# Threshold attention and an MLP mixer on one core: identity turns that wait for a bank, and second-layer visits of 256 features

## The chip, the core and the metric

The kernel runs on one core of a Trainium2 chip. The metric is the device time of one execution in microseconds (us). The engines go by their short names: PE is TensorE (matrix products; PEld is its weight loads), DVE is VectorE, ACT is ScalarE, POOL is GpSimd, SP is the engine whose queue starts most transfers. All data are f32. A matrix product of f32 shows in the profile as two PE instructions ("passes"), each with its own weight load, so that 12 products are 24 passes.

## What is computed

Attention with a threshold (B=8 rows, H=8 heads, S=576 tokens, D=64), then a mixer on the 8 rows of 576 tokens by 512 features:

```python
scores = scale * q @ k.T                         # per row and head
scores = where(scores >= max(scores) - tau, scores, -1e9)
x = softmax(scores) @ v                          # heads side by side: (8, 576, 512)
h = relu(x.T @ w_tok1) @ w_tok2                  # token layers: 576 -> 256 -> 576
u = x + h.T
out = u + relu(u @ w_ch1) @ w_ch2                # channel layers: 512 -> 1536 -> 512
```

## The kernel before

**Stages.** The rows go through attention one after the other. While PE does the attention of row b+1, it also does the token layers and one or two channel groups of row b; that other work fills PE where attention waits for ACT, DVE or POOL. A channel group is 256 tokens of one row through both channel layers. `NOW` (L524) says how many groups of a row are done in this way: two of row 0, one of each of rows 1 to 6, none of row 7, eight in all. The rest is done at the end, from 903 us on, by `class Late` (L1250), in another scheme with 256-wide products; the diff doesn't touch it.

**A channel group** (`make_groups`, L919). First layer: 12 visits (`ch1`, L944), each 4 products of 128x128 weights by 256 tokens into one bank, then a relu on ACT (L953) or DVE (L956) into `g`. Second layer: `ch2` (L958). A visit takes 128 tokens `t` and 128 output features `c`; it is 12 products, one for each block `j` of the hidden layer: the weights are a 128x128 block of `g`, and what is streamed is 128 columns of `wc2` (L964). In row 0 a product with the identity ahead of them adds `u` (L962). A group has 2 x 4 = 8 such visits. `leave` (L973) takes the bank out: in row 0 a copy on ACT (L984), in the other rows an addition on DVE (L978) of the bank and of `ut`, which holds u turned to tokens by features; then `store` (L986) writes 128 tokens to `out`, once the four visits of a `t` have left. `ut` comes from `turn_u`, a DVE transpose (L933) into the buffer `us`, which must wait until the stores of the group before have read `us`, and from four moves in SP's queue (L940).

**Banks.** A visit to PE that leaves something in PSUM needs a bank. Until attention ends there are two, `m0` and `m1` (L707); two more come afterwards (L1216). Who needs one: the turns of attention's weights in row 0 (L300), attention's value products (L365, L370), the token layers (L435, L454, L472) and both channel layers. The scores (L825) have banks of their own.

**The order of the work** is written by a planner at build time (`class Scheduler`, L568 on). Every piece of work is an `Op` with an engine, a cost in us, a function that emits its instructions, what it depends on, and a rank (low goes first). `banked` (L591) makes two: the visit on PE, which takes a bank as it starts, and its leaving, which gives the bank back 0.15 us after its end. The planner keeps one clock for each engine and emits, over and over, the piece that can start first; among those that PE can start now, `pick` (L617) puts first those whose inputs and bank have been there for about a microsecond (`sure`, L598: a piece on the same engine counts 0.2 us after the end of what it needs), then the lowest rank. Ranks on PE: value products 0, scores 1 (-1 in row 0), token layers 1.5, or 2.5 right after another token piece, channel layers 2. A round of scores is moreover held back while the other work done so far, `self.done` (L694: the costs of banked visits that belong to a row), is below the round's due value (`planned_at`, L1165, worked out with `GROUP` = 41.8 for a group), as long as something else can start. On the chip each engine then works through its own instructions in the emitted order.

**Turns of the identity** (`keep_warm`, L647). Before a piece is put on PE that starts before 110 us of the planner's clock (`WARM_UNTIL`, L550), the gap ahead of it is filled with transposes of the identity that nobody reads. There are as many as fit in the gap less `WARM_GAP` = 0.6 us, at 0.11 us each. They need a bank, and are left out if none is free at the moment at which PE's gap begins.

Of the kernel before, what the change touches and what calls it, by code (L numbers as in the profile page):

```python
# [17 lines left out]
P = 128  # L18
# [3 lines left out]
def kernel(  # L22
# [38 lines left out]
    NCC = DM // P  # L61
    NJ = DCH // P
# [7 lines left out]
    work = ctx.enter_context(tc.tile_pool(name="work", bufs=2))  # L70
# [74 lines left out]
    wc2 = const.tile([P, NJ, DM], F32, name="wc2")  # L145
# [233 lines left out]
    class Step:  # L379


        def __init__(self, kind, cost, on, cost_out, work, leave, other=None):
            self.kind, self.cost, self.on, self.cost_out, self.work, self.leave = kind, cost, on, cost_out, work, leave
            self.other = other
# [167 lines left out]
    class Op:  # L552

        def __init__(self, eng, cost, fn, deps, after, rank, lag, row, index):
            self.eng, self.cost, self.fn, self.rank, self.lag, self.row, self.index = eng, cost, fn, rank, lag, row, index
            self.end, self.bank, self.frees, self.later, self.open, self.other = None, None, None, [], 0, None
            self.dmas, self.landed, self.shared = None, None, False
            self.deps = [d for d in deps if d is not None]
            for d in self.deps + [d for d in after if d is not None]:
                if d.end is None:  # L560
                    d.later.append(self)
                    self.open += 1
# [5 lines left out]
    class Scheduler:  # L568
# [22 lines left out]
        def banked(self, cost, work, on, cost_out, leave, deps=(), rank=5, row=None, rank_out=0, other=None):  # L591
            x = self.op("pe", cost, work, deps, rank, row=row)
            y = self.op(on, cost_out, leave, (x,), rank_out, row=row, other=other)
            x.bank = True
            y.frees = x
            return x, y

        def sure(self, x):  # L598
            t = max([d.landed + SPARE if d.landed else d.end + d.lag + SLACK * (d.eng != x.eng) for d in x.deps] + [0.0])
            if x.bank:  # L600
                t = max(t, min(b.free for b in self.banks if b.free is not None) + SLACK)
            return t
# [44 lines left out]
        def keep_warm(self, t):  # L647

            now = self.clock["pe"]
            banks = [b for b in self.banks if b.free is not None and b.free <= now]  # L650
            n = int((t - now - WARM_GAP) / WARM_TURN)
            if not banks or n < 1 or not now:
                return
            b = banks[0]
            to = b.pool.tile([P, MAIN], F32, tag=b.tag, name=f"warm_{len(self.warmed)}")
            for _ in range(n):
                nc.tensor.transpose(out=to[:, 0:P], in_=ident, identity=ident)
            self.clock["pe"] = now + n * WARM_TURN
            b.free = self.clock["pe"] + 0.15
            self.warmed.append((now, n))  # L660

        def run(self, until):
            while not until():
                best = None
                for e in self.clock:
                    c = self.pick(e)
                    if c and (best is None or c[0][0] < best[0][0]):
                        best = c + (e,)
                if best is None:
                    assert all(x.end is not None for x in self.ops), [(x.eng, x.rank, x.index, x.open) for x in self.ops if x.end is None][:20]  # L670
                    return
                _, t, x, eng = best
                if eng == "pe" and t < WARM_UNTIL:
                    self.keep_warm(t)
                self.ready[x.eng].remove(x)
                if x.other:
                    self.ready[x.other[0]].remove(x)
                    if eng != x.eng:
                        x.eng, x.cost, x.fn = x.other
                if x.dmas:  # L680
                    x.end = self.transfer(t, *x.dmas)
                    x.landed = self.in_flight[-1]
                else:
                    x.end = t + x.cost
                self.clock[x.eng] = x.end
                if x.eng == "pe":
                    self.last_rank = x.rank
                if x.bank:
                    b = min((b for b in self.banks if b.free is not None), key=lambda b: b.free)
                    b.free = None  # L690
                    x.bank = b, b.pool.tile([P, MAIN], F32, tag=b.tag, name=f"bank_{x.index}")
                    x.fn(x.bank[1])
                    if x.row is not None:
                        self.done += x.cost  # L694
                elif x.frees:
                    b, tile_ = x.frees.bank
                    x.fn(tile_)
                    b.free = x.end + 0.15
                else:
                    x.fn()  # L700
                for y in x.later:
                    y.open -= 1
                    if not y.open:
                        self.enter(y)

    sched = Scheduler()
# [3 lines left out]
    def key_op(*key):  # L710
        return keyed.get(key)
# [165 lines left out]
    fills = {}  # L877
# [41 lines left out]
    def make_groups(b, halves):  # L919
        uT = xTs[b]  # L920
        reads = []
        for i in range(NOW[b]):
            s = {}
            n, nt = GR, GR // P

            def new_us(s=s, i=i):
                s["us"] = work.tile([P, nt, 4, NCC * 32], F32, tag="us", bufs=1, name=f"us_{b}_{i}")
# [27 lines left out]
            def relu_v(bank, j, s=s):  # L955
                nc.vector.tensor_scalar(out=s["g"][:, j, 0:n], in0=bank[:, 0:n], scalar1=0.0, scalar2=None, op0=ALU.max)  # L956

            def ch2(bank, t, c, s=s, i=i):  # L958
                to = bank[:, 0:P]
                t0 = GR * i + P * t  # L960
                if not b:
                    nc.tensor.matmul(to, lhsT=uT[:, c, t0 : t0 + P], rhs=ident, is_transpose=True, start=True, stop=False, skip_group_check=True)  # L962
                for j in range(NJ):
                    nc.tensor.matmul(  # L964
                        to,
                        lhsT=s["g"][:, j, P * t : P * t + P],
                        rhs=wc2[:, j, P * c : P * c + P],
                        start=(j == 0 and b > 0),
                        stop=(j == NJ - 1),
                        skip_group_check=True,  # L970
                    )

            def leave(bank, t, c, s=s):  # L973
                if not b and "us" not in s:
                    new_us(s)
                o = s["us"][:, t].rearrange("q a x -> q (a x)")[:, P * c : P * c + P]
                if b:
                    nc.vector.tensor_add(  # L978
                        out=o.rearrange("q (k d) -> q k d", k=4),
                        in0=bank[:, 0:P].rearrange("q (k d) -> q k d", k=4),  # L980
                        in1=s["ut"][:, t][:, :, 32 * c : 32 * c + 32],
                    )
                else:
                    nc.scalar.copy(out=o, in_=bank[:, 0:P])  # L984
# [12 lines left out]
            for j in range(NJ):  # L997
                x, y = sched.banked(
                    1.79,
                    lambda bank, j=j, f=ch1: f(bank, j),  # L1000
                    "act",
                    0.29,
                    lambda bank, j=j, f=relu: f(bank, j),
                    have + state["ch2"] + [key_op("pool", 7 + j)],
                    2,
                    b,
# [5 lines left out]
            seconds, stores, adds = [], [], []  # L1012
            for t in range(nt):
                outs = []
                for c in range(NCC):
                    x, y = sched.banked(
                        2.7 if b else 2.8,
                        lambda bank, t=t, c=c, f=ch2: f(bank, t, c),
                        "dve" if b else "act",
                        0.21,  # L1020
                        lambda bank, t=t, c=c, f=leave: f(bank, t, c),
                        relus + moved + (converted if not b else []) + (state["stores"] if not b else []),
                        2,
                        b,
                        1 if b else 0,
                    )
                    outs.append(y)
                    seconds.append(x)
                    if not b:
                        reads.append(x)  # L1030
                    fills[b] = fills.get(b, 0.0) + x.cost
                adds += outs
                stores.append(sched.op("sp", 0.35, lambda t=t, f=store: f(t), outs, 2, dmas=(1, 150, 0.35)))
            state["ch2"], state["stores"], state["adds"] = seconds, stores, adds
# [453 lines left out]
```

## Time and profile before

| | us |
|---|---|
| three runs: median (lowest to highest) | 1270.09 (1269.9 to 1276.9) |
| the profiled execution: its own time | 1273.39 |
| its span, from the first to the last instruction | 1271.4 |
| PE busy in the span | 1237.8 |
| DVE, ACT, POOL busy | 755.0, 564.0, 315.4 |
| mean granted clock of PE | 0.991 of full |
| end of the last second-layer visit | 903.3 |

Lines of the profile name the engine, the source line (L964 is the product of `ch2`), the tile written and the tiles read. A timeline line is: start, length, engine, line, operation, what is written and read, how many, and in brackets the idle time ahead of it with what ended it. The table of windows gives, for each stretch of time, its length, then the busy time and number of instructions of PE, PEld, DVE, ACT and POOL, then PEclk, the share of the full clock that PE was granted, then DMA's share and GB/s. The chain of waits follows what ended last back to the start, and lists its pieces in order of time as start, length and what ran.

### The profile page before, as it was taken

What the parts mean: (1) busy time and instruction counts of PE and PEld (TensorE: products, weight loads), DVE (VectorE), ACT (ScalarE), POOL (GpSimd) and SP (SyncE); (2) the same over time, 40 slices, a digit from 0 to 9 for tenths busy, and PEclk for the clock granted to TensorE, in tenths of its full rate; (3) what the DMA queues carried; (4) which work ended last, traced back from release to release, by engine and by line L of the source; (5) the groups of instructions that cost most, each with busy time, mean ns of one, the idle gap of its engine ahead of it and who ended that gap; (6) DMA issues with size and microseconds to landing.
All of it is one profiled execution on the core that took longest, in us unless ns stands there. A gap on an engine that the chain in (4) does not pass through costs nothing.

```text
span 1271.4 us, 21773 instructions
## 1 busy us (share of the span) xinstructions
PE 1237.8 (97%) x8150; PEld 1015.3 (80%) x8150; DVE 755.0 (59%) x1163; ACT 564.0 (44%) x1233; POOL 315.4 (25%) x518
## 2 busy tenths in 40 slices
PE   8888999999999999999989999999999999999998
PEld 7656778797678778878867777888988888888887
DVE  6699982656666667756666756761443534444443
ACT  6998862554645545556465455531110202011120
POOL 4565641232223333323323322410001010000100
PEclk9899999999999999999999999999999999999999
DMA  9546985366777786786776875750212101021011
GB/s 167 139 124 166 214 212 131 87 128 160 168 164 175 160 169 150 165 178 137 179 148 135 187 159 111 179 150 1 60 23 67 34 25 42 18 67 25 26 34 33
DMA packets 324216, 149.23 MB, mean 117 GB/s; under 512 B 223696, under 2 KB 316880, under 8 KB 324112
## 3 DMA queue, kind: packets, MB, share of 16 engines
q1 hardware_dynamic: 322240, 147.64, 50.5%
q8 instruction: 64, 1.05, 0.4%
q10 hardware_dynamic: 1872, 0.21, 0.1%
q14 instruction: 40, 0.33, 0.1%
HBM read 47.32 MB, written 13.50 MB: 48 GB/s over the span
## 4 chain that ended last, share of the span: by engine, by line
PE 78%; SPq 6%; DVE 5%; DMA 5%; ACT 4%; issue 2%; POOL 0%; DVEq 0%; ACTq 0%; POOLq 0%
PE bank L964 11%; PE bank L948 10%; PE o L1309 10%; PE sc L825 9%; PE bank L370 7%; PE hx L1309 6%; PE bank L454 5%; PE hmm L1309 4%; PE oz L1309 4%; PE hz L1309 4%; PE bank L472 4%; SPq L327 3%; PE bank L365 2%; DVE mx L842 2%; ACT e L858 2%
## 5 line engine op out<-in xcount | busy, mean ns | idle before, releaser
L285 POOL TENSOR_SCALAR e<-e,rr 128x576 f32<-128x576 f32 x288 | 213.2, 758 | 299.1 <-DVE rr L277 286.6
L858 ACT ACTIVATE e<-sc,bias 128x576 f32<-128x576 f32 x288 | 194.1, 740 | 156.8 <-POOL bias L848 155.1
L842 DVE TENSOR_REDUCE mx<-sc 128x2 f32<-128x1152 f32 x144 | 188.1, 1347 | 58.9 <-PE sc L825 58.4
L868 ACT ACTIVATE e<-e,ntau 128x576 f32<-128x576 f32 x288 | 220.4, 778 | 0.3
L315 DVE STREAM_TRANSPOSE T<-e 128x1152 f32<-128x1152 f32 x126 | 170.0, 1362 | 36.1 <-POOL e L285 22.2
L948 PE MATMUL bank<-xT,wc 128*128 128x256 f32 x768 | 181.0, 389 | 6.1 <-ACT g L953 5.1
L964 PEld LDWEIGHTS bank<-wc,g 128*128 128x128 f32 x1536 | 178.0, 192 | 10.4 <-issue 2.4
L964 PE MATMUL bank<-wc,g 128*128 128x128 f32 x1536 | 181.4, 276 | 0.9 <-DVE xT L483 0.4
L948 PEld LDWEIGHTS bank<-xT,wc 128*128 128x128 f32 x768 | 144.2, 192 | 36.6 <-ACT g L953 6.5
L825 PE MATMUL sc<-kT,qT 64*128 64x192 f32 (+1 forms) x1920 | 168.8, 337 | 2.7 <-ACT e L858 2.7
L825 PEld LDWEIGHTS sc<-kT,qT 64*128 64x128 f32 (+1 forms) x1920 | 140.8, 179 | 32.1 <-issue 16.3
L370 PE MATMUL bank<-eT,lv 128*64 128x384 f32 (+1 forms) x1024 | 135.2, 406 | 0.0
L1392 POOL TENSOR_TENSOR us<-us,ut 128x256 f32<-128x256 f32 x27 | 22.4, 843 | 391.8 <-DVE us L1230 391.8
L370 PEld LDWEIGHTS bank<-eT,lv 128*64 128x64 f32 x1024 | 74.4, 137 | 49.7 <-issue 41.3
L848 POOL TENSOR_SCALAR bias<-mx,toff 128x2 f32<-128x2 f32 x144 | 38.8, 270 | 197.9 <-DVE mx L842 193.3
L454 PE MATMUL bank<-x_sb,w 128*128 128x256 f32 x320 | 72.8, 383 | 0.3 <-DVE eT L305 0.2
L472 PE MATMUL bank<-w,a 128*128 128x192 f32 (+1 forms) x256 | 72.8, 418 | 0.2 <-DVE xT L483 0.2
L454 PEld LDWEIGHTS bank<-x_sb,w 128*128 128x128 f32 x320 | 59.8, 190 | 11.3 <-issue 1.3
L953 ACT ACTIVATE g<-bank 128x256 f32<-128x256 f32 x66 | 25.3, 383 | 92.9 <-PE bank L948 92.7
L1357 ACT ACTIVATE ga<-hmm 128x256 f32<-128x256 f32 x30 | 11.5, 384 | 116.8 <-PE hmm L1309 116.8
L1230 DVE TENSOR_TENSOR temps<-hx,temps 128x256 f32<-128x256 f32 x60 | 25.1, 418 | 56.7 <-PE hx L1309 56.6
L868 ACT ACTIVATION_READ_ACCUMULATOR e<-e,ntau 128x1 f32 x288 | 58.4, 203 | 0.0
(133 smaller groups left out, 1519.6 us busy)
## 6 DMA issues: line engine op xcount, KB each, us to landing
eT<-T SPq DMA_DIRECT2D x504, 144.0 KB, 3.0
lk<-in_k_dram SPq DMA_DIRECT2D x126, 72.0 KB, 2.9
lq<-in_q_dram SPq DMA_DIRECT2D x124, 72.0 KB, 3.1
out_dram<-us SPq DMA_DIRECT2D x32, 256.0 KB, 2.1
ut<-us SPq DMA_DIRECT2D x128, 64.0 KB, 2.1
lv<-in_v_dram SPq DMA_DIRECT2D x112, 72.0 KB, 2.6
spare<-in_moe_w_ch_dram SPq DMA_DIRECT2D x8, 512.0 KB, 3.9
extra<-in_moe_w_ch_dram SPq DMA_DIRECT2D x8, 512.0 KB, 3.8
```

The costliest lines, as they stand in the source:

```text
L285: nc.gpsimd.tensor_scalar(out=eh, in0=eh, scalar1=rr[:, h : h + 1], scalar2=1.0, op0=ALU.mult, op1=ALU.mult)
L315: nc.vector.transpose(out=T.rearrange("p a (c x) -> p c a x", c=NK), in_=e.rearrange("p (c a x) -> p c a x", c=NK, a=4))
L370: nc.tensor.matmul(to[r], lhsT=lv[:, j, :], rhs=e[j], start=False, stop=(c == NI - 1), skip_group_check=True)
L454: nc.tensor.matmul(to, lhsT=w1[:, t, P * m : P * m + P], rhs=x(t), start=(t == 0), stop=(t == NT - 1), skip_group_check=len(products) > 1,)
L472: nc.tensor.matmul(bank[:, n * i : n * i + n], lhsT=hidden[b][:, m, P * c : P * c + P], rhs=w2[:, m, lo : lo + n], start=(m == 0), stop=(m ...
L825: nc.tensor.matmul(sc[h][rows, f, HT * k : HT * k + HT], lhsT=qT[r, cols], rhs=kT[r, HT * f : HT * f + HT], start=True, stop=True, skip_gr ...
L842: nc.vector.tensor_reduce(out=mx[:, h], in_=sc[h][:, :, 0 : 2 * HT].rearrange("p f (k x) -> p k f x", k=2), axis=AX.XY, op=ALU.max)
L858: nc.scalar.activation(out=eh, in_=part[h], func=AF.Prelu, bias=bias[:, h], scale=SCALE, alpha=STEEP)
L868: nc.scalar.activation(out=eh, in_=eh, func=AF.Exp, bias=ntau, accum_out=rs[:, h, 0:1])
L948: nc.tensor.matmul(bank[:, 0:n], lhsT=wc1[:, j, c, :], rhs=uT[:, c, GR * i : GR * i + n], start=(c == 0), stop=(c == NCC - 1))
L964: nc.tensor.matmul(to, lhsT=s["g"][:, j, P * t : P * t + P], rhs=wc2[:, j, P * c : P * c + P], start=(j == 0 and b > 0), stop=(j == NJ - 1 ...
L1309: nc.tensor.matmul(ps, lhsT=l, rhs=r, start=start and x == 0, stop=x == len(pairs) - 1, skip_group_check=not start)
```

## The change

Two things change.

First, `keep_warm` no longer asks for a bank that is free at the start of the gap. It takes the bank that comes free first, and lets the turns begin at that moment, if it is later than the start of the gap; their number is worked out from there.

Second, in rows 1 to 6 a second-layer visit covers 256 output features in place of 128 (`wide` = 2): 12 products with 256 streamed columns, a leaving of 128x256 with a planned cost of 0.35 in place of 0.21, four visits in a group in place of eight. Such a visit is made by the new `banked_in_two`: two pieces on PE of 6 products each, planned at 2.6 us each (before: 2.7 for a visit of 12 products by 128). The first piece takes the bank, and the second goes on in the same bank; it needs no new one, has a rank 0.1 lower than the first, and other work can come between the two. The leaving waits for the second. Both pieces count in `self.done`, the second by the new flag `counts`. Row 0 keeps its visits of 128. `GROUP` and the due values are as before.

```diff
+        def banked_in_two(self, cost, work, on, cost_out, leave, deps, rank, row, rank_out):
+            x = self.op("pe", cost, lambda bank: work(bank, 0), deps, rank, row=row)
+            z = self.op("pe", cost, lambda: work(x.bank[1], 1), (x,), rank - 0.1)
+            z.counts = True
+            y = self.op(on, cost_out, leave, (z,), rank_out, row=row)
+            x.bank = True
+            y.frees = x
+            return z, y
...
         def keep_warm(self, t):
             now = self.clock["pe"]
-            banks = [b for b in self.banks if b.free is not None and b.free <= now]
+            banks = [b for b in self.banks if b.free is not None]
+            if not banks or not now:
+                return
+            b = min(banks, key=lambda b: b.free)
+            now = max(now, b.free)
             n = int((t - now - WARM_GAP) / WARM_TURN)
-            if not banks or n < 1 or not now:
+            if n < 1:
                 return
-            b = banks[0]
...
                     x.fn()
+                    if x.counts:
+                        self.done += x.cost
...
+            wide = 2 if b else 1
+            def ch2(bank, t, c, half=None, s=s, i=i, wide=wide):
-                to = bank[:, 0:P]
+                to = bank[:, 0 : wide * P]
...
-                for j in range(NJ):
+                for j in range(NJ) if half is None else range(NJ // 2 * half, NJ // 2 * half + NJ // 2):
                     nc.tensor.matmul(
                         to,
                         lhsT=s["g"][:, j, P * t : P * t + P],
-                        rhs=wc2[:, j, P * c : P * c + P],
+                        rhs=wc2[:, j, P * c : P * c + wide * P],
...
                 if b:
                     nc.vector.tensor_add(
-                        out=o.rearrange("q (k d) -> q k d", k=4),
-                        in0=bank[:, 0:P].rearrange("q (k d) -> q k d", k=4),
-                        in1=s["ut"][:, t][:, :, 32 * c : 32 * c + 32],
+                        out=o.rearrange("q (w k d) -> q w k d", w=wide, k=4),
+                        in0=bank[:, 0 : wide * P].rearrange("q (w k d) -> q w k d", w=wide, k=4),
+                        in1=s["ut"][:, t].rearrange("q k (c d) -> q c k d", c=NCC)[:, c : c + wide],
                     )
...
-                for c in range(NCC):
-                    x, y = sched.banked(
-                        2.7 if b else 2.8,
-                        lambda bank, t=t, c=c, f=ch2: f(bank, t, c),
+                for c in range(0, NCC, wide):
+                    make = sched.banked_in_two if b else sched.banked
+                    x, y = make(
+                        2.6 if b else 2.8,
+                        lambda bank, *half, t=t, c=c, f=ch2: f(bank, t, c, *half),
                         "dve" if b else "act",
-                        0.21,
+                        0.35 if b else 0.21,
```

More of the change, by code (lines that the diff above doesn't have):

```diff
@@ L556, in __init__ @@
             self.end, self.bank, self.frees, self.later, self.open, self.other = None, None, None, [], 0, None
-            self.dmas, self.landed, self.shared = None, None, False
+            self.dmas, self.landed, self.shared, self.counts = None, None, False, False
             self.deps = [d for d in deps if d is not None]
@@ L956, in relu_v @@
                 nc.vector.tensor_scalar(out=s["g"][:, j, 0:n], in0=bank[:, 0:n], scalar1=0.0, scalar2=None, op0=ALU.max)
-            def ch2(bank, t, c, s=s, i=i):
-                to = bank[:, 0:P]
+            wide = 2 if b else 1
+            def ch2(bank, t, c, half=None, s=s, i=i, wide=wide):
+                to = bank[:, 0 : wide * P]
                 t0 = GR * i + P * t
@@ L971, in ch2, with leave @@
                     )
-            def leave(bank, t, c, s=s):
+            def leave(bank, t, c, s=s, wide=wide):
                 if not b and "us" not in s:
                     new_us(s)
-                o = s["us"][:, t].rearrange("q a x -> q (a x)")[:, P * c : P * c + P]
+                o = s["us"][:, t].rearrange("q a x -> q (a x)")[:, P * c : P * c + wide * P]
                 if b:
                     nc.vector.tensor_add(
-                        out=o.rearrange("q (k d) -> q k d", k=4),
-                        in0=bank[:, 0:P].rearrange("q (k d) -> q k d", k=4),
-                        in1=s["ut"][:, t][:, :, 32 * c : 32 * c + 32],
+                        out=o.rearrange("q (w k d) -> q w k d", w=wide, k=4),
+                        in0=bank[:, 0 : wide * P].rearrange("q (w k d) -> q w k d", w=wide, k=4),
+                        in1=s["ut"][:, t].rearrange("q k (c d) -> q c k d", c=NCC)[:, c : c + wide],
                     )
@@ L1030, in make_groups @@
                         reads.append(x)
-                    fills[b] = fills.get(b, 0.0) + x.cost
+                    fills[b] = fills.get(b, 0.0) + x.cost * wide
                 adds += outs
```

## The prediction

> **What bounds the kernel now.** I read the page first, then PE's time by stage in the table of windows, then the chain of waits, and then the timeline at the places where PE stands still.
>
> ```profile
> span 1271.4 us, 21773 instructions
> PE 1237.8 (97%) x8150; PEld 1015.3 (80%) x8150; DVE 755.0 (59%) x1163; ACT 564.0 (44%) x1233; POOL 315.4 (25%) x518
> PEclk9899999999999999999999999999999999999999
> ```
> ```profile
> 140.00:903.00 763.00, 750.04 (x5561) 602.89 (x5560) 481.08 (x675) 391.70 (x858) 214.78 (x366) 1.00 0.66 149
> 903.00:1271.40 368.40, 363.16 (x1683) 319.21 (x1681) 158.97 (x292) 54.40 (x130) 22.40 (x27) 1.00 0.14 38
> ```
>
> PE is the bound: of the 763 us in which rows 1 to 6 are worked off it stands still for 13. DVE and ACT have room there (481 and 392 of 763). What shortens PE's work between 140 and 903 us shortens the kernel; the last 368 us are not touched by the diff. Row 0, ahead of 140 us, is different: from 16 to 112 us PE, ACT and DVE are busy for 84, 85 and 81 us of 96, and the chain of waits goes through all three and through transfers. The clock row has its one 8 there, and finer windows show why:
>
> ```profile
> 26.45:29.86 3.41, 1.99 (x11) 1.02 (x9) 3.38 (x7) 3.16 (x8) 1.21 (x6) 1.00 1.29 188
> 29.86:33.28 3.42, 2.75 (x17) 2.71 (x18) 1.49 (x5) 3.42 (x9) 2.93 (x4) 0.50 0.67 124
> 33.28:36.69 3.41, 3.41 (x17) 2.64 (x16) 2.50 (x2) 1.64 (x6) 1.43 (x5) 0.50 0.32 103
> 53.76:57.17 3.41, 1.49 (x11) 0.88 (x9) 3.16 (x4) 3.41 (x9) 1.78 (x4) 1.00 0.71 196
> 57.17:60.58 3.41, 2.04 (x8) 1.64 (x8) 2.56 (x9) 3.18 (x8) 1.54 (x2) 0.50 0.03 3
> 111.78:115.20 3.42, 2.16 (x14) 1.41 (x14) 3.13 (x4) 2.83 (x6) 3.19 (x6) 1.00 0.48 153
> 16.40:22.30 5.90, 5.90 (x54) 5.77 (x53) 5.73 (x10) 5.90 (x15) 3.46 (x6) 1.00 0.87 171
> 640.85:644.26 3.41, 3.17 (x8) 2.52 (x8) 1.44 (x2) 3.41 (x8) 0.00 (x0) 0.50 0.71 182
> ```
>
> Behind the five busy times stands PE's granted clock. Windows of 4 us (0.73, 0.50 and 0.91 from 28 to 40) place the first halved stretch at 29.86 to 36.69; the second is as long, and the one at 640.85 half as long, so I cut the time into pieces of 3.41 us. Twice in row 0 the clock is halved for 6.8 us, both times behind a piece in which PE was busy for under 2.0 us; behind one of 2.16 (111.78) it stayed whole.
>
> **Visits of 256: PE's work.** The price of a pass comes from two lines of the chain of waits, in which PE runs without a break:
>
> ```profile
> 892.57 10.73 PE bank L964 x96
> 940.20 5.18 PE o L1309 x24
> ```
>
> A pass with 128 columns takes 10.73/96 = 0.1118 us; one with 256, into the same kind of bank, 5.18/24 = 0.2158. Rows 1 to 6 have six groups of eight visits, which become 24 visits of 24 passes. Each takes 24 x 0.2158 = 5.18 in place of 2 x 24 x 0.1118 = 5.37, a saving of 0.185 us, 4.4 us in all. It lies in the stretch where PE is the bound, so I count it whole. From below: first-layer visits mixed with other work show 5.38 for 24 passes of 256, which would leave nothing; but that extra 0.2 comes once for each of three visits of eight passes, some 0.07 at a visit's start. From above: 24 visits fewer save that start as well, 1.6 more, 6.0 in all. The L1309 row has the same shape, twelve products into one bank, so 4.4 is taken, between 0 and 6.0.
>
> **Visits of 256: leaving.** DVE's 48 additions of 128x128 at 275 ns (13.2 us) become 24 of 128x256. The late stage's addition with the same second operand (128x256, us<-o,ut) takes 425 ns: 10.2 us. DVE gains 3.0 us, which is worth nothing while it idles 282 of the 763 us; nor would it cost if it went the other way. The one place on the path is the last visit, at 903.33, whose addition of 0.30 holds up the late stage: +0.1. Each store still waits for the last addition of its 128 tokens, and that comes at the same point of the work; the number and size of the transfers stay.
>
> **Visits of 256: the bank.** A pair now holds a bank from the first half's start to the addition behind the second, 5.2 + 0.4 us at the least, where it was 2.7 + 0.3. By the planner's rule the second half is not "sure" at the moment that the first ends (0.2 us after its end is later than now), so any other sure piece goes first, another first half too: both banks can be held at once. Queued behind that are value products, token layers and the next group's first layer; for them wait the copies on ACT and DVE, T's buffers, and the transfers behind these in SP's queue. What covers it: a second half needs no new bank, so PE has 2.6 us of work for each bank held. I take 0. From below: PE's waits for a bank in this stretch, 0.9 + 1.0 + 0.4 + 0.7 + 0.6 (L948, L365, L964, L435) could go, 3.6. From above: if the cover fails, a stall like the worst one of before, next.
>
> ```profile
> 631.60 2.79 DMA out_dram<-us
> 641.09 3.55 PE L948 MATMUL bank<-xT,wc 128*128 128x256 f32 x8 [2.60 <-ACT g L953]
> ```
>
> There a store stood in SP's queue behind other issues, `turn_u` on DVE waited for it, the maxima and relus behind it came late, and PE stood for 2.60 us with both banks full. The clock was then halved for 3.4 us with 3.17 busy, 1.6 lost: 4.2 us a stall. It happens twice (the other at 746 us).
>
> **Due times.** A group's planned second layer is 8 x 2.6 = 20.8 in place of 21.6, and the due values stay, so scores are held 0.8 us of work longer for each row done, 4.8 by the last. That costs nothing while filling work is left: four visits (892.57) still stood alone on PE at the very end. Without that cover it is at most 4.8 us, once.
>
> **Turns.** They are added only where PE waits for something other than the bank; where it waits for the bank (most of row 0's waits: 5.6 us for copies on ACT, 2.4 on DVE), the gap ends as the bank comes free. What is left are the waits of scores for ACT, 2.7 us over five places. The one that matters:
>
> ```profile
> 28.48 0.98 DVE L305 COPY eT<-bank 128x384 f32<-128x384 f32 x2
> 29.31 0.59 PE L825 MATMUL sc<-kT,qT 64*128 64x192 f32 x2 [0.83 <-ACT e L858]
> 30.57 4.21 PE L825 MATMUL sc<-kT,qT 64*128 64x192 f32 x22 [0.67 <-ACT e L858]
> 55.77 0.98 PE L300 MATMUL bank<-ident,e 128*128 128x128 f32 x6 [1.51 <-ACT eT L305]
> ```
>
> The first of the two copies ends near 29.0 and frees a bank; the scores can go on in full at 30.57. That leaves 1.5 - 0.6 = 0.9 us, eight turns of 0.11. Of these some 0.3 us net fall before 29.86, and would bring the 1.99 busy us to about 2.3, above the 2.16 at which the clock held. The 22 scores then take about 2.1 us less (24 take 2.22 at full clock, here 22 took 4.21), and they are on the chain of waits. I take -2.1. Ahead of the second halved stretch PE waits for banks (the 55.77 line), so it stays. From below: both stretches whole, (2.75 + 3.41 + 2.04 + 3.42)/2 = -5.8. From above: turns planned into a gap that is shorter on the chip push the scores back; the same five waits over again are +2.7.
>
> The Trainium skill, TensorE: Matmul & The Clock Gate, Part 4 (PE-mode transpose), says that a transpose doesn't count as PE-busy for the clock in the way a product does. By that the turns would buy nothing and the row 0 term would be 0. The trace speaks against it: from 16.40 to 22.30 PE ran almost only turns and the clock stayed 1.00. The table at that page's end asks only that no idle gap exceed about 3 us; here the clock halved with no gap over 1.51 us in the 3.4 us ahead, so the measurement decides, and short gaps count.
>
> **The sum.** -4.4 + 0.1 - 2.1 = -6.4. Against the profiled execution (1273.4, 2.0 us of it outside the span) that is 1267.0. The median of the runs is 3.3 lower, 1270.1, so 1263.7.
>
> **Rivals.**
> - *The turns do nothing:* no gap is long enough by the planner's clock, or the runs of 1270 had already kept the clock that the profiled one lost (one halved stretch costs 3.1, and they are 3.3 apart). For it: most waits are for banks. 1270.1 - 4.3 = 1265.8. Chance 0.25. The skill's rule on transposes would end here too.
> - *More goes than was meant:* both halved stretches and one of the two stalls of 4.2 vanish, since new lengths move the rows' ends. -4.3 - 5.8 - 4.2 gives 1255.8. Against it: the second stretch stands behind bank waits. Chance 0.14; this is all of "faster by over 1%" (under 1257.4).
> - *Banks held through both halves stall PE:* value products and token layers find both banks taken, their copies come late, and PE stands with no second half left. At 4.2 a stall it decides against the saving of 4.3 from the second stall on; three give 1270.1 - 4.3 + 12.6 = 1278.4. For it: DVE, which empties these banks, is up to 2.6 us behind at such places, and with one bank left nothing is double-buffered. Against it: second halves fill in. Chance 0.19, of it 0.08 beyond 1282.8 (four stalls or more).
>
> The forecast has the other 0.42, with a range of its own of 1260 to 1268. The whole range, 1256 to 1278, cuts the two outer rivals in their middles and leaves out some 0.16. One per cent, 12.7 us, is about what a measurement of this kernel can tell from no change: faster 0.14, same 0.78, slower 0.08.
>
> **What would show it.** L964 with 576 passes of 256 columns at 0.216 and 384 of 128 (row 0) at 0.112, and the last visit ending near 897. More turns than 98, a few of them ahead of the scores near 29 us, and a granted clock of 1.00 from 30 to 36 us. In the list of waits, PE's waits of L365, L454, L472 and L948 for copies at no more than before. The forecast is wrong if L964's total saves under 3 us, if PE's idle time between 140 and 903 us grows past 17 us (13 now), or if a halved stretch comes more often than four times.

## The result and the profile after

| | before | changed |
|---|---|---|
| median of 6 runs each, us | 1271.89 (1269.9 to 1276.9) | 1261.89 (1261.1 to 1266.5) |
| ratio, 95% interval | | 0.9926 (0.9902 to 0.9951) |
| again, 28 and 9 runs | 1269.23 | 1262.85 |
| ratio, 95% interval | | 0.9942 (0.9922 to 0.9961) |
| profiled execution: own time, span | 1273.39, 1271.4 | 1261.13, 1259.4 |

The forecast was 1263.7, or -6.4 us. Measured by the ratios are -9.4 (-12.4 to -6.2) and, with more runs, -7.4 (-9.9 to -4.9). That is within 1% of before and clearly on the fast side. The changed kernel's two medians are 1 us apart; what differs is before, which stood at 1271.9 in six runs and at 1269.2 to 1269.7 in the 87 runs of the experiments, so the first ratio is rather too good. One run of before among the experiments, of 1300.17 us, was in a slower state and is in none of the medians and ratios here.

The page of the changed kernel, against the three lines shown of before:

```profile
span 1259.4 us, 20636 instructions
PE 1228.2 (98%) x7590; PEld 989.2 (79%) x7590; DVE 751.7 (60%) x1136; ACT 565.3 (45%) x1236; POOL 316.1 (25%) x518
PEclk9999999999999999999999999999999999999999
```

PE is still the bound, busy for 9.6 us less, and the 8 of the clock row is gone. The lines by form show PE's second layer (L980; it was L964) and DVE's addition (L994), and the chain of waits the last visit:

```profile
L980 PE MATMUL bank<-wc,g 128*128 128x256 f32 x576 | 133.0, 381 | 2.6 <-ACT g L967 2.3 <-ACT x_sb L439 0.2
L980 PE MATMUL bank<-wc,g 128*128 128x128 f32 x384 | 45.2, 275 | 0.0
L994 DVE TENSOR_TENSOR us<-bank,ut 128x256 f32<-128x256 f32 x24 | 10.0, 415 | 34.3 <-PE bank L980 32.6 <-DMA lq<-in_q_dram 1.6
```
```profile
889.01 2.59 PE bank L980 x12
891.60 0.86 PE hmm L1326 x4
```

There are 576 passes of 256 and row 0's 384 of 128, as forecast; 12 passes take 2.59 us, 0.216 each. By the start of its first product the late stage comes 12.2 us earlier than before (903.7 to 891.4), and it is as long as before, 368 us. In the timeline of PE, the place at 29 us now reads:

```profile
28.98 1.20 PE L669 MATMUL warm<-ident 128*128 128x128 f32 x9 [0.58 <-DVE eT L305]
30.11 2.60 PE L839 MATMUL sc<-kT,qT 64*128 64x192 f32 x24
```
```profile
26.45:29.86 3.41, 2.25 (x17) 1.54 (x16) 3.38 (x7) 3.16 (x7) 1.25 (x6) 1.00 1.32 207
32.00:36.00 4.00, 2.81 (x23) 1.99 (x20) 3.56 (x5) 3.68 (x10) 2.99 (x7) 1.00 0.68 169
```

Nine turns stand there (eight were forecast), PE is busy for 2.25 us from 26.45 to 29.86 (2.3 forecast), and the clock is whole from 32 to 36 us, where before it was 0.50. The 24 score passes end at 32.7, where before they ended at 34.8. The pieces of 3.41 us that fit this run's halved stretch lie elsewhere, at 24.49, 27.91 and 31.32; PE is busy for 2.60, 2.83 and 2.44 us in them. Three more turns stand near 46 us and four near 57, 16 in all.

### The profile page after: what moved, and what is told of

It is laid out like the page before. It is cut to its first block, busy times and chain, and to the rows that moved or that the text cites. A ratio compares the mean times of both kernels' runs of the same rounds, so it can differ in the third digit from the quotient of the medians.

```text
span 1259.4 us, 20636 instructions
## 1 busy us (share of the span) xinstructions
PE 1228.2 (98%) x7590; PEld 989.2 (79%) x7590; DVE 751.7 (60%) x1136; ACT 565.3 (45%) x1236; POOL 316.1 (25%) x518
## 4 chain that ended last, share of the span: by engine, by line
PE 79%; DVE 6%; SPq 4%; DMA 3%; ACT 2%; issue 1%; POOL 0%; DVEq 0%; POOLq 0%
PE bank L980 12%; PE o L1326 10%; PE bank L962 10%; PE sc L839 9%; PE bank L370 8%; PE hx L1326 6%; PE bank L472 4%; PE hz L1326 4%; PE oz L1326 4%; PE hmm L1326 4%; PE bank L454 4%; PE bank L365 2%; SPq L327 2%; DVE mx L856 2%; DMA eT<-T 1%
## 5 line engine op out<-in xcount | busy, mean ns | idle before, releaser
L980 PE MATMUL bank<-wc,g 128*128 128x256 f32 (+1 forms) x960 | 178.2, 339 | 2.6 <-ACT g L967 2.3
L962 PE MATMUL bank<-xT,wc 128*128 128x256 f32 x768 | 178.0, 385 | 2.5 <-ACT xT L374 2.0
L980 PEld LDWEIGHTS bank<-wc,g 128*128 128x128 f32 x960 | 152.4, 191 | 26.3 <-issue 4.8
L839 PE MATMUL sc<-kT,qT 64*128 64x192 f32 (+1 forms) x1920 | 165.9, 334 | 0.6 <-ACT e L872 0.5
L1247 DVE TENSOR_TENSOR temps<-hx,temps 128x256 f32<-128x256 f32 x60 | 25.1, 418 | 56.7 <-PE hx L1326 56.6
```

The lines of the kernel that those rows point to most:

```text
L839: nc.tensor.matmul(sc[h][rows, f, HT * k : HT * k + HT], lhsT=qT[r, cols], rhs=kT[r, HT * f : HT * f + HT], start=True, stop=True, skip_gr ...
L962: nc.tensor.matmul(bank[:, 0:n], lhsT=wc1[:, j, c, :], rhs=uT[:, c, GR * i : GR * i + n], start=(c == 0), stop=(c == NCC - 1))
L980: nc.tensor.matmul(to, lhsT=s["g"][:, j, P * t : P * t + P], rhs=wc2[:, j, P * c : P * c + wide * P], start=(j == 0 and b > 0), stop=(j == ...
```

## The experiments

The twelve runs form three series, each beside before, whose medians were 1269.56 (30 runs), 1269.23 (28) and 1269.66 (29); the second series was on another chip than the other two, so kernels of different series are compared by their ratios to before. A difference of two ratios is uncertain by some 0.0025, or 3 us. In the traces the order of work on every engine is the same for before and for the turns alone but for the turns, and so it is for the changed kernel and the visits alone: the first edit moves no other work, and the turns cannot act by another plan.

**The turns alone, twice.** Only `keep_warm` as in the diff, visits of 128.

> Before, with the first edit alone: turns begin when a bank comes free. The emitted order of all other work is that of before; 16 turns are added (9 ahead of the scores near 29 us, 3 near 46, 4 near 57). Theory: the turns keep the clock whole in row 0 and the scores that came at 127.7 us come some 4.8 us earlier; 1271.9 - 4.8 = 1267. Rival (the ten us come nearly all from rows 1 to 6, by stalls that went): no more than 2 us, 1270. Rival (turns push the scores back): above 1272.

Measured: 1269.79, ratio 0.9998 (0.9984 to 1.0012). The second time, below: 1.0009 (0.9995 to 1.0023). Alone the turns bring nothing, though in the first of its profiles the scores that came at 127.71 in the profile of before come 4.8 us earlier, as the theory had it. Its time did not follow. The time is that of the first rival (no more than 2 us, 1270), but its reason, stalls that went in rows 1 to 6, is not seen: both profiles of this kernel have three halved stretches there, before's has two.

**The visits alone, twice.** The changed kernel with `keep_warm` of before.

> After, without the first edit: the visits of 256 alone, in the emitted order of the changed kernel, with the 98 turns of before. Theory: 4.4 from the passes and up to 1 from waits, 1266.5 to 1267.5; the two gains add up to the ten measured. Rival (new lengths move the rows' ends and stalls go): 8 or more, 1264 or less. Rival (the two edits need one another): above 1269.

Measured: 1265.57, 0.9967 (0.9952 to 0.9982). The second time 0.9971 (0.9954 to 0.9988). These are 4.2 and 3.7 us; the forecast's -4.3 for the visits holds. The median is 0.9 us below the range that was expected, which was reckoned from the slower before of the first result.

**Narrow passes in the new order.**

```diff
-                to = bank[:, 0 : wide * P]
+                to = bank[:, 0:P]
...
-                for j in range(NJ) if half is None else range(NJ // 2 * half, NJ // 2 * half + NJ // 2):
+                if half is not None:
+                    to, c = bank[:, P * half : P * half + P], c + half
+                for j in range(NJ):
...
-                        rhs=wc2[:, j, P * c : P * c + wide * P],
+                        rhs=wc2[:, j, P * c : P * c + P],
```

> The changed kernel with each half of a wide visit doing all 12 products for one of its two 128 columns (24 passes of 128) in place of 6 products of 256 (12 passes of 256). Order, banks, the leaving of 128x256 and the turns are those of the changed kernel; only the passes are narrow. Theory: the visits' gain is the passes', 24 x 0.185 = 4.4 back, 1261.9 + 4.4 = 1266.3. Rival (the gain is the new order, fewer additions or a stall that went): 1262 to 1263.

Measured: 1267.65, 0.9977 (0.9958 to 0.9996). Against the changed kernel's 0.9942, from the next series, that is 4.4 us back, what the passes were to cost; by the intervals it could be 1 to 8 us. The trace is sharper. A half of a visit, alone on PE, takes 2.68 us here, where it takes 2.59 in the changed kernel (the line at 889.01 above), which is 4.3 us over 48 halves:

```profile
896.81 2.68 PE bank L982 x24
```

**Nine turns only.** The seven turns near 46 and 57 us are left out.

```diff
+            late = b.free > now
             now = max(now, b.free)
             n = int((t - now - WARM_GAP) / WARM_TURN)
-            if n < 1:
+            if n < 1 or (late and now > 31.0):
                 return
```

> The changed kernel with only the nine turns near 29 us added, not the seven near 46 and 57 us. Theory: the nine keep the first stretch whole and so move all behind it, and the second stretch goes with its place in time or is rarely there; 1262 to 1263. Rival (the second stretch needs its own four turns): a halved stretch near 57 us remains, 2.7 more, 1264.6.

Measured: 1264.92, 0.9957 (0.9940 to 0.9974), between the visits alone and the changed kernel, and not clear of either. In its profile the stretch near 30 us is gone and the one at 58.2 is there, as the rival had it.

**The changed kernel again.**

> The changed kernel once more, beside before on this chip, where before stands at 1269.7, the turns alone gave 0.9998 and the visits alone 0.9967. Theory: the edits add up, the visits give 4.2, the turns 0 to 2.5 on average (they keep the clock whole in some runs and not in others), so 1263 to 1265.5; the ten us first measured came from few runs of before and after. Rival (the edits need one another): 1260 to 1261, as first measured.

Measured: 1262.85, 0.9942. That is 0.15 under the theory's range, and the rival's 1260 to 1261 is not reached.

**A visit in one piece.**

```diff
-                    make = sched.banked_in_two if b else sched.banked
-                    x, y = make(
-                        2.6 if b else 2.8,
+                    x, y = sched.banked(
+                        5.2 if b else 2.8,
...
-                    fills[b] = fills.get(b, 0.0) + x.cost * wide
+                    fills[b] = fills.get(b, 0.0) + x.cost
```

> The changed kernel with each visit of 256 as one piece of 5.2 us on PE in place of two halves of 2.6; passes, leaving and turns unchanged, the planner's order is another. Theory: the gain is the passes', so within 1.5 us of the changed kernel. Rival (a half that needs no bank is what keeps PE busy; without it PE waits at the ends of rows): 4 us or more above it.

Measured: 1269.14, 0.9991 (0.9972 to 1.0011), 6.3 us above the changed kernel in the same series. The rival's time holds: all that the change brought is lost. Three lines of PE's waits from 140 to 905 us, of this kernel first and of the changed one second:

```profile
PE bank L962 <- DVE g L970: 6.7, 3, 3.4
PE bank L365 <- DMA x_sb<-extra: 2.9, 1, 2.9
PE bank L472 <- DVE xT L483: 1.6, 2, 1.2
```
```profile
PE bank L365 <- DMA x_sb<-extra: 2.2, 1, 2.2
PE bank L962 <- DVE g L970: 0.5, 2, 0.3
PE bank L472 <- DVE xT L483: 0.3, 1, 0.3
```

The first layer of the next group stands with both banks full until DVE gets to the relu (L970), and waits 6.2 us more than in the changed kernel, by its first profile. Other waits are shorter, so that PE's waits come to 17.1 us in all against 11.6. The timeline of the worst place, at 730 us of the kernel in one piece:

```profile
727.47 2.58 DVE L856 TENSOR_REDUCE mx<-sc 128x2 f32<-128x1152 f32 x2
729.97 0.41 DVE L970 TENSOR_SCALAR g<-bank 128x256 f32<-128x256 f32 x1
730.44 6.78 PE L962 MATMUL bank<-xT,wc 128*128 128x256 f32 x16 [3.42 <-DVE g L970]
```

The relu stood behind two maxima in DVE's queue, and the 16 passes behind it, which took 3.62 us at full clock in the profile of before (729.75), took 6.78. That a half without a bank would have filled this very wait is argued; the planner's order differs in other places too.

**Turns without a bank.** The turns go into the unused last 128 columns of a scores bank and start with the gap.

```diff
-            now = max(now, b.free)
...
-            to = b.pool.tile([P, MAIN], F32, tag=b.tag, name=f"warm_{len(self.warmed)}")
+            to = tops[max(tops)][0][0][:, 0, MAIN - P : MAIN]
...
-            b.free = self.clock["pe"] + 0.15
```

> The changed kernel with its turns written into the unused last 128 columns of a scores bank, so that they need no bank and start with the gap: 24 turns more by the count of the emitted order near 25 to 60 us, the order of all else as in the changed kernel. Theory (row 0's halved clock is what the turns act on, and PE's time there is on the path): mean granted clock higher than the changed kernel's, time 1 to 2.5 us less. Rival (row 0's PE time is covered by ACT, DVE and transfers): clock higher, time the same. Rival (turns push the scores back): time above the changed kernel's.

Measured: 1278.21, 1.0065 (1.0046 to 1.0084), 15 us above the changed kernel, but not for the rival's reason as I meant it: the experiment missed its aim. The turns, 152 of them in the profile in place of 114, waited for the readers of the scores' tile (the two largest of all waits of PE in this kernel):

```profile
PE sc L666 <- ACT e L868: 11.6, 9, 4.3
PE sc L666 <- DVE w L227: 3.1, 1, 3.1
```

The scores behind the turns came late too: the second group of 24 passes, which starts at 14.13 in the changed kernel, starts at 20.71 here, behind 44 turns. It shows only what a turn costs that starts late.

**Stores first.** The rank of the stores is -2 in place of 2; the planner's order of the other work changes with it.

> The changed kernel with the planner's rank of the output stores set to go first in SP's queue. Theory (at a row's end the transpose of u waits for a store that stands behind other transfers, and PE's longest waits of 2 us with a halved clock behind them follow from that): these waits go, 2 to 6 us less than the changed kernel. Rival (another transfer is then the late one, the moves that the stores now precede): no difference, or up to 3 us more.

Measured: 1261.26, 0.9935 (0.9914 to 0.9956), 1.6 us under the changed kernel, with intervals that overlap for the most part. In its profile PE waited 3.0 us for relus and copies in the channel layers, where the changed kernel waited 5.0 in its first; but L365 waited 7.0 us for transfers, where the changed kernel's two profiles have 3.8 and 4.8. So the rival, that another transfer is then the late one, fits the waits; a gain of 1.6 us, under what the theory asked for, isn't clear of noise either way.

**No turns at all.** All 114 are left out; the order of the rest stays.

> The changed kernel without any turn of the identity behind the first 24, neither the 98 of before nor the 16 added; the order of all other work is the same. Theory (row 0's clock is on the path): the halved stretches come from 9 us on, as many as three or four in row 0, mean clock under 0.992, and row 0's end comes at 122.9 + 0.37 for each halved us, 129 or more; 6 us or more above the changed kernel. Rival (row 0's PE time is covered, so that turns hardly matter, as the turns alone gave 0.9998): the clock falls, the time by less than 3 us.

Measured: 1267.39, 0.9984 (0.9965 to 1.0002), 5 us above the changed kernel by the ratios. The clock fell to 0.9886 on average (0.9954 for the changed kernel). The windows of this kernel:

```profile
9.49:12.90 3.41, 0.28 (x2) 0.28 (x2) 3.34 (x5) 2.79 (x5) 0.71 (x2) 1.00 1.29 265
12.90:26.60 13.70, 10.24 (x58) 7.17 (x59) 9.00 (x14) 11.66 (x27) 7.21 (x11) 0.50 1.29 196
```

The clock was halved for 24 us of row 0 in three stretches. Yet the 13th round of scores came only 5.4 us later than with a whole clock (128.30 against 122.86): the truth lies between the two theories. Much of PE's time in row 0 is covered by other engines.

**Turns alone and visits alone again, in one series.**

> Before with the first edit alone, once more, beside the visits alone and before in one call. Theory (a gain in those runs in which the turns avoid a halved stretch, 2.5 us for each of 6.8 us): 1 to 3 us under before, clock 0.997 against 0.994. Rival (the turns are worth nothing on average): 0.9998 again.

> The changed kernel without the first edit, once more, beside the turns alone and before. Theory: 0.9967 again within its interval, 4 to 5 us under before; the changed kernel's 0.994 then leaves 2 to 3 us to the turns. Rival (the visits give nearly all): 0.9945 or less.

Measured: 1270.71 and 1266.18, given above. The rival holds for the turns by themselves, the theory for the visits, whose 3.7 us fall just short of its 4 to 5.

**Stores first without the new turns.**

> The visits alone with the output stores first in SP's queue: the kernel with stores first (0.9935), less the 16 added turns; the order of all else is the same. Theory (the turns are worth 2 to 3 us beside the visits): 0.9955 to 0.996. Rival (worth nothing): 0.9935 again.

Measured: 1262.62, 0.9943 (0.9925 to 0.9962), against 0.9935 with the turns: 1.0 us, with intervals wider than that. The forecast of 0.9955 or more failed. Stores first thus brings 3.3 us on the visits alone and 0.9 on the changed kernel; the first is barely clear of noise, the second not.

## Why the prediction was right, and where it was not

Here is every profile but that of the turns without a bank, with the start and length of the halved stretches of row 0, the start of the 13th round of scores (the fourth of row 1, taken here for the end of row 0's attention), and the time from the 18th round to the late stage. This time is split into PE's idle time, what the halved clock cost (an estimate: half of PE's busy time in the halved stretches, since 22 score passes took 4.21 us there and 24 take 2.22 at full clock), and the rest, which is PE's work at full clock.

| kernel | turns | halved in row 0, us | 13th round | 18th to late | idle | lost to clock | work |
|---|---|---|---|---|---|---|---|
| before | 98 | 29.9: 6.8; 57.2: 6.8 | 127.71 | 711.0 | 13.3 | 3.3 | 694.4 |
| turns alone | 114 | none | 122.94 | 712.0 | 13.1 | 5.1 | 693.8 |
| turns alone, again | 114 | 57.7: 6.8 | 126.52 | 712.8 | 14.0 | 5.1 | 693.6 |
| visits alone | 98 | 31.8: 3.4; 55.7: 6.8 | 125.34 | 703.8 | 12.9 | 1.7 | 689.2 |
| visits alone, again | 98 | 30.0: 3.4; 57.3: 6.8 | 126.31 | 707.1 | 13.2 | 4.8 | 689.2 |
| stores first, no new turns | 98 | 30.8: 3.4; 58.1: 6.8 | 125.76 | 703.1 | 12.4 | 1.7 | 689.0 |
| nine turns | 107 | 58.2: 6.8 | 125.27 | 703.6 | 11.3 | 3.4 | 688.8 |
| changed | 114 | none | 122.86 | 703.0 | 12.0 | 1.7 | 689.3 |
| changed, again | 114 | 56.7: 6.8 | 125.40 | 705.5 | 12.9 | 3.4 | 689.2 |
| stores first | 114 | none | 122.82 | 703.1 | 12.5 | 1.7 | 689.0 |
| one piece | 114 | none | 122.84 | 710.5 | 17.3 | 4.8 | 688.4 |
| narrow passes | 114 | 55.8: 10.2 | 126.54 | 707.5 | 10.8 | 3.4 | 693.3 |
| no turns | 0 | 12.9: 13.7; 33.4: 3.4; 60.7: 6.8 | 128.30 | 703.4 | 11.1 | 3.4 | 688.8 |

**PE is the bound, and a pass of 256 saves 0.185 us a visit: right.** The pass is 0.216 us as read from the late stage's row, and the visits alone bring 3.7 to 4.2. In the table, PE's work is 693.6 to 694.4 us with visits of 128, 688.8 to 689.3 with visits of 256 in halves, and 693.3 with narrow passes in the new order: 4.0 to 5.6 us, in every profile, whatever the clock did. The busy time of the line itself, which was to show it, is a poor measure: with row 0's passes it fell from 181.4 to 178.2 us in the first profile, but to 179.9 only in the second, since it holds overlapping ends of passes and time at half clock. The upper bound of 6.0 took it that a wide visit has one start in place of two, worth 1.6 us in all. In halves it still has two. In one piece it has one, and there PE's work is 0.4 to 0.9 us less than in halves.

**Leaving: right, and small.** DVE's additions took 415 ns, not 425, 10.0 us in all. The +0.1 at the last visit is not seen: the late stage follows the last visit with no wait in the chain, and the 0.4 us for which PE waited there before is gone too.

**The bank at 0: right, but its cover was needed.** The forecast took 0 because a second half needs no bank, and kept as a rival that banks held through a visit stall PE. In one piece, stalls of that kind do come (a visit waits for a bank, DVE late, clock halved), and the kernel is 6.3 us slower, more than the passes save: in the table its idle time is 4.4 to 5.3 us longer than the changed kernel's, and it loses 1.4 to 3.1 us more to the clock. In halves, PE's idle time from 140 us to the late stage is 12 to 13 us, as before.

**The turns, -2.1: right at the place and for the profile that was read, but neither stretch is fixed.** At the place the forecast came true: the scores end 2.1 us earlier. The nine turns take away the first stretch in every profile that has them, and against the profile of before the 13th round comes 2.4 us earlier with nine turns alone (127.71 to 125.27). But that profile had 6.8 us of halved clock there. The three others with 98 turns, whose work up to 355 us is that of before in the same order, had 3.4, and against these the nine turns bring only 0.1 to 1.0 us. What did not hold is "so it stays", said of the second stretch. It is absent in four of the seven profiles with all 16 turns and present in all six of the others, and where it is absent the 13th round comes 2.3 us earlier or more. Windows show when. The first two lines are of the changed kernel's second profile, the last two of its first:

```profile
53.29:56.70 3.41, 1.68 (x12) 1.21 (x12) 3.38 (x5) 3.41 (x10) 0.89 (x3) 1.00 0.45 109
56.70:60.12 3.42, 3.25 (x16) 2.53 (x16) 1.99 (x8) 3.42 (x9) 3.18 (x4) 0.50 0.18 33
```
```profile
51.80:55.21 3.41, 2.04 (x16) 1.26 (x12) 3.14 (x4) 3.41 (x9) 1.84 (x4) 1.00 0.71 198
55.21:58.63 3.42, 2.50 (x16) 1.74 (x18) 2.91 (x9) 3.42 (x8) 2.26 (x2) 1.00 0.00 0
```

It is the same program. In the one run the quiet time near 55 us falls into one piece of 3.41 us, with 1.68 busy, and the clock is halved behind it; in the other the border at 55.21 cuts it into 2.04 and 2.50, and the clock stays. So the turns do not decide the second stretch alone; where the pieces lie in that run does as well. The four turns near 57 us often come too late for it: in the three profiles with 16 turns and a second stretch they start at 57.3, 58.2 and 58.4, behind the border at which the clock was halved. The second of these, in the turns alone, where the stretch starts at 57.7:

```profile
58.16 1.11 PE L660 MATMUL warm<-ident 128*128 128x128 f32 x4 [0.32 <-DVE eT L305]
```

**The sum** came out within 1.8 us of both medians, and of the change it gave 6.4 us where 9.4 and 7.4 were measured. Between the two profiles first shown the span fell by 12.0: 4.2 up to the 18th round, 8.0 from there to the late stage (5.1 work, 1.6 clock, 1.3 idle), and 0.2 back in the late stage. That is a good run set beside a poor one. The profiled run of before had a clock of 0.991, the 87 runs of the experiments 0.9937 on average, so what the first rival held possible, that the usual runs "had already kept the clock that the profiled one lost", was so in part. That the -2.1, read from this one profile, came near what the runs gave is partly luck.

Beside the visits the turns bring 3.4 us by the ratios (0.9942 against 0.9967 and 0.9971), near the 2.1 of the forecast but barely clear of noise. The clock goes with it: the runs' mean was 0.9930 and 0.9926 for the visits alone, 0.9963 and 0.9954 for the changed kernel, and over the 87 runs of before 0.001 more of clock goes with 0.9 us less. Alone they bring 0, with stores first 1.0. Why they bring nothing alone stays open. It is not the 13th round in the profiled run, which was 4.8 us earlier; both profiles of the turns alone have three halved stretches in rows 1 to 6 (near 339, 640 and 745 us); before's has two. Over its runs the mean clock was better than before's in the first series (0.9962 against 0.9938) and the same in the third (0.9942 against 0.9940), with the same time in both. Before has a single profile, 3.7 us above its usual median, so I can't say in which rows its usual run is quicker than this one.

**Due times** were not tried.

## What to carry to other kernels

Read a saving in PE passes from a row that runs without a break, and then ask who holds the banks: the same passes in one piece, in the order that the planner then wrote, brought nothing, in halves that need no new bank 4 us. Work that fills a gap must be done when real work is ready: the turns that waited for readers of the scores' tile cost 15 us. A clock stretch that is halved is worth what the chain behind it loses, which one profile can't tell where the stretch comes and goes from run to run.

## What the hardware showed

- I cut 13 profiles into the pieces of 3.41 us that fit each one's halved stretches. From a whole clock, it was halved behind every piece with under 1.50 us of PE busy time (28 pieces) and behind none with 2.01 or more. In between it seems to go by the work: in row 0, where PE mostly did transposes in groups of three, it was halved behind pieces of 1.66 to 2.00 and held behind two of 1.87; in rows 1 to 6, where it did products, it held behind all but one from 1.51 to 1.96. The Trainium skill (TensorE: Matmul & The Clock Gate, Part 1) describes such a window of 3.4 us that runs freely; the two profiles of one program above agree with it.
- Turns without a break held the clock: with them it was 1.00 from 16.40 to 22.30, without them 0.50 from 12.90 to 26.60. That transposes count for less than products would fit the row 0 pieces; that they count for nothing doesn't fit the turns. Part 4 of that page of the Trainium skill (PE-mode transpose) says that the full clock doesn't engage for a transpose; here it did, with 54 instructions of PE in a row, nearly all turns, and the measurement decides.
- 24 us of halved clock in row 0 moved the 13th round of scores by only 5.4 us. That other engines cover the rest fits row 0, where from 16 to 112 us PE, ACT and DVE were busy for 84, 85 and 81 us in the profile of before.
